# One list scheduler in the source for every engine and every transfer of an attention and feed-forward kernel

## The chip, the core and the metric

The kernel runs on one core of one Trainium2 chip. The metric is the device time of one execution in microseconds (us). The kernel before was run three times: 918.08, 918.18 and 919.11 us, median 918.18. A further execution was recorded by the profiler; every row below is from that one.

## The reference

Eight sequences of 576 tokens with eight heads of 64 go through a sparse attention: heads 0 to 3 look back over 32 tokens, heads 4 to 7 look at every 32nd token. The result, 4608 tokens of 512 values, goes through two matrices with a silu between them.

```python
scores = scale * np.matmul(q, k.transpose(0, 1, 3, 2))
mask_local = (rel >= 0) & (rel < stride)                      # heads 0..3, stride 32
mask_strided = (rel >= 0) & (pos[None, :] % stride == pos[:, None] % stride)
scores = np.where(masks[None, :, :, :], scores, -1000000000.0)
attn = np.exp(scores - np.max(scores, axis=-1, keepdims=True))
attn = attn / (np.sum(attn, axis=-1, keepdims=True) + 1e-09)
x = np.matmul(attn, v)            # then (4608, 512)
h = x @ w_in                      # (512, 2048)
out = (h * (1.0 / (1.0 + np.exp(-h)))) @ w_out
```

## The kernel before

**Attention.** A sequence has six groups, so there are 48 groups, numbered c. Of the six, 0 to 2 are local and 3 to 5 strided. A group goes through these steps, and the text names them by letters: S, the scores (TensorE, L380); M, mask and row minimum (VectorE, L396); E, the exponentials (ScalarE, L403); R, sum and reciprocal (VectorE, L422 and L423), and N, for strided groups only, the scaling of the weights (VectorE, L427); T, the transposition on TensorE (L433); P, its copy out of PSUM (ScalarE, L437); O, the product with the values (TensorE, L445 local, L453 strided). A local group then has Q, a scaling (VectorE, L463), and B, 16 transpositions of 32x32 blocks on VectorE (L499, `blocks`); a strided one has a ScalarE copy (L476). The trace shows two records for one attention matmul, the listed order one.

**Feed-forward.** Numbers are kept in two halves, a rounded high part and a low rest, so each product is three matmuls of 128x128 weights with 512 columns. Tokens come in nine blocks of 512.

- Stage 1 (block 0, to about 138 us): weights come in by 32 pieces and are split; the attention of sequences 0 and 1 runs beside it.
- Stage 2 (blocks 1 and 2, to about 395 us): for each of 16 chunks of the hidden layer there is a hidden step h (12 matmuls into PSUM, L529), then the silu chain tanh on ScalarE (L539), gate (VectorE, L543), high part (L552) and low part (VectorE, L556), and one chunk later the output step o (12 matmuls, L576). Beside it, 18 groups of attention run in bursts, and sums of weight blocks are prepared for stage 3: GpSimd adds two blocks (`summed`, L820, twice) and makes four sums (L825 to L828); ScalarE rounds a half (`halved`, L834), it is stored (L835), VectorE takes the rest (L836), and it is stored (L837); both again for the other half. There are 16 such rounds with one buffer, and each round's parts follow each other. Unchanged weight blocks are stored too (`plain`, L815, six stores of 128 KB a round, 96 in all).
- Stage 3 (blocks 3 to 8 in three pairs, by seven products in place of eight for each layer): 12 matmuls a step (L1044 first layer, L1089 second layer), weights read back in units of 1 MB (`load_unit`, L866), operands built on ScalarE and VectorE (L904, L906, L912, L968, L976), results stored from L1105.

**What sets the order.** In stage 1 a list scheduler in the source (`Steps`, `arrange`) places the steps of all engines by estimated costs and due times. From `others.close()` on, TensorE's and SyncE's queues take the order in which the source is written: in stage 2 h, o, the stores of `prepare`, and where `plan` says so a `burst(c)`, which is T of c+1, S of c+2, O of c. For VectorE, ScalarE and GpSimd the framework chooses the order there. Each engine works off its queue in order.

```python
    def burst(c):
        turn(c + 1)
        scores(c + 2)
        values(c)
        total(c + 2)
```

Of the kernel before, what the change touches and what calls it, by code (L numbers as in the profile page):

```python
# [102 lines left out]
SIGNAL = 0.2  # L103


class Step:
    def __init__(self, name, costs, due, after, act):
        self.name, self.costs, self.due, self.act = name, costs, due, act
        self.engine, self.after = None, list(after)
        self.takes, self.ends, self.place = [], {}, {}  # L110
        self.writes, self.start, self.end = [], None, None


class Steps:
# [3 lines left out]
    def __init__(self):  # L118
        self.all, self.rings, self.by_name = [], {}, {}
        self.readers, self.taken = collections.defaultdict(list), collections.defaultdict(list)  # L120

# [19 lines left out]

    def ready(self, step):

        at = 0.0
        for other in step.after:
            if other.end is None:
                return None
            at = max(at, other.end + (SIGNAL if other.engine != "SP" else LANDING))
        for ring in step.takes:
            if len(self.taken[ring]) >= self.rings[ring]:  # L150
                for other in self.taken[ring][-self.rings[ring]].ends[ring]:
                    if other.end is None:
                        return None
                    at = max(at, other.end + SIGNAL)
        return at

    def arrange(self):
        free = collections.defaultdict(float, SP=1.3, DVE=6.0, ACT=7.6, POOL=6.8)
        left, order = list(self.all), []
        while left:  # L160
            could = []
            for step in left:
                if (at := self.ready(step)) is not None:
                    ways = [(max(free[e], at), e, cost) for e, cost in step.costs.items()]
                    at, engine, cost = min(ways, key=lambda way: way[0] + way[2])
                    could.append((at, step, engine, cost))
            now = min(c[0] for c in could)
            soon = [c for c in could if c[0] <= now + 0.05]
            at, step, step.engine, cost = min(soon, key=lambda c: c[1].due)
            step.start, step.end, step.cost = at, at + cost, cost  # L170
            free[step.engine] = step.end
            for ring in step.takes:
                self.taken[ring].append(step)
            left.remove(step)
            order.append(step)
        return order
# [3 lines left out]
def sparse_attention_ffn(ctx: ExitStack, tc: tile.TileContext, kqt, vt, w_in, w_out, out, out_t):  # L180
# [172 lines left out]
    class Attention:  # L353
# [31 lines left out]
        def peak(self):  # L385
# [7 lines left out]
            for c in range(g.n):  # L393
                for h in range(2):
# [7 lines left out]
                    if not self.quick:  # L402
                        nc.scalar.activation(  # L403
                            out=s_sb[:, c, h], in_=s_sb[:, c, h], func=AF.Exp,
                            bias=nmax[:, c, h : h + 1], scale=-1.0,
                            accum_out=rsum[:, c, h : h + 1],
                        )
# [82 lines left out]
        def blocks(self):  # L490
# [6 lines left out]
            for t, d in itertools.product(range(n), range(n)):  # L497
# [6 lines left out]
    def parts(k, cc):  # L504
        at = k * T
        while at < (k + 1) * T:
            b = at // S
            n = min((b + 1) * S, (k + 1) * T) - at
            if (k, b) == (2, 1):
                yield carry[:, cc, at - k * T : at - k * T + n], slice(at - k * T, at - k * T + n)  # L510
# [225 lines left out]
    for step in steps.arrange():  # L736
        step.act()
    others.close()

    due = [(kind, j) for j in range(2 * NG, len(groups)) for kind in "kv"]  # L740
    due = [what for what in due if what not in (("k", 2 * NG), ("k", 2 * NG + 1))]
    scored, weighed = set(range(2 * NG + 2)), set(range(2 * NG))

    def load_due():

        while due:
            kind, j = due[0]
            bufs, load_one, read = (KBUFS, load_qk, scored) if kind == "k" else (
                VBUFS, load_v, weighed)
            if j - bufs not in read:  # L750
                return
            load_one(groups[j].b, groups[j].gi)
            due.pop(0)
# [3 lines left out]
    def scores(c):  # L757
        if c < len(groups):
            groups[c].scores()
            scored.add(c)  # L760
            load_due()
            groups[c].peak()

    def total(c):
        if c < len(groups):
            groups[c].total()
            if not groups[c].g.local:
                groups[c].scale()

    def turn(c):  # L770
        if c < len(groups):
            groups[c].turn()
            groups[c].turned()

    def values(c):
        if c < len(groups):
            groups[c].values()
            weighed.add(c)
            load_due()
            if groups[c].g.local:  # L780
                groups[c].share()
                groups[c].blocks()
            else:
                groups[c].sorted()
# [14 lines left out]
    ops_dram = [[dram.tile([7, P, 4, 2, Q], F32, name=f"ops{layer}{half}") for half in range(2)]  # L799
                for layer in range(2)]  # L800
    raw = ffn.tile([P, 4, Q], F32, name="stage", bufs=AHEAD - LENT)
    spare = ffn.tile([P, 2, 2, Q], F32, name="stage", bufs=AHEAD - LENT)
    upper = spare[:, 0].bitcast(F32R)
    carry = spare[:, 1].rearrange("p a b -> p (a b)").rearrange("p (c s) -> p c s", c=NP)
    nc.gpsimd.tensor_copy(out=carry, in_=xs[1][:, :, 2 * T - S :])
# [5 lines left out]
    def plain(layer, j):  # L811
        for name, fc, at in (("A11", j, 0), ("A12", j + HALF if layer else j, 0 if layer else Q),
                             ("A22", j + HALF, Q)):
            for half in range(2):
                load(out=where(layer, name, j)[:, half],  # L815
                     in_=weight(layer, half, fc)[:, at : at + Q].bitcast(F32))

    def summed(layer, j):
        for n, fc in enumerate((j, j + HALF)):
            nc.gpsimd.tensor_add(  # L820
                raw[:, 2 * n : 2 * n + 2].rearrange("p a q -> p (a q)"),
                weight(layer, 0, fc).bitcast(F32), weight(layer, 1, fc).bitcast(F32),
            )
        a11, a12, a21, a22 = (raw[:, n] for n in ((0, 2, 1, 3) if layer else (0, 1, 2, 3)))
        nc.gpsimd.tensor_add(a22, a21, a22)  # L825
        nc.gpsimd.tensor_sub(a21, a11, a21)
        nc.gpsimd.tensor_sub(a11, a22, a11)
        nc.gpsimd.tensor_sub(a12, a12, a11)  # L828

    def halved(layer, j, n):  # L830
        kept = ops_dram[layer][j // 4]
        part = raw[:, 2 * n : 2 * n + 2]
        to = kept[3 + 2 * n : 5 + 2 * n, :, j % 4].rearrange("a p h q -> p a h q")
        nc.scalar.copy(out=upper, in_=part)  # L834
        load(out=to[:, :, 0], in_=upper.bitcast(F32))  # L835
        nc.vector.tensor_sub(out=part, in0=part, in1=upper.bitcast(F32))  # L836
        load(out=to[:, :, 1], in_=part)  # L837

    def prepare(k, fc):
        layer, j = k - 1, fc // 2  # L840
        last = (layer, j - 1) if j else (layer - 1, HALF - 1)
        if fc % 2 == 0:
            if last[0] >= 0:
                halved(*last, 1)
            summed(layer, j)
        else:
            plain(layer, j)
            if (layer, j) != (1, HALF - 1):
                halved(layer, j, 0)
# [8 lines left out]
    unit_names = ("w00_5", "w00_9", "w01_12")  # L858
    unit_tiles = {}
    used = [0]  # L860

    def load_unit(n):
# [383 lines left out]
```

## Time and profile before

| | |
|---|---|
| three runs, us | 919.11, 918.08, 918.18 |
| the profiled execution, us | 920.54 |
| its span from first to last instruction, us | 918.8 |
| TensorE busy in the span | 94% |
| VectorE, ScalarE, GpSimd busy | 67%, 50%, 13% |
| mean granted TensorE clock | 0.976 |

The profiled execution took 920.54 us, of which 918.8 lie between its first and its last instruction. A row of the timeline has start, duration, engine, line, operation, tile written and read, shape and count, and in brackets how long the engine sat idle before it and what it then waited for. A row of the windows has the length, then for PE, PEld (its weight loads), DVE (VectorE), ACT (ScalarE) and POOL (GpSimd) the busy time and the number of instructions, then the granted clock (PEclk), the share of time in which the DMA engines were busy, and GB/s. SPq is SyncE issuing transfers.

### The profile page before, as it was taken

Reading aid. Unit: us, or ns where it says so; the run is one execution under the profiler, and the core shown is the slowest. Engines: PE = TensorE matmul, PEld = TensorE weight load, DVE = VectorE, ACT = ScalarE, POOL = GpSimd, SP = SyncE. Lnnn points to the kernel's source line nnn. Section 1 sums busy time; section 2 is a strip of 40 time slices with the busy share of each in tenths; the row PEclk is TensorE's granted clock in tenths of the full one; section 3 lists DMA queues with packets and bytes.
Section 4 is the critical chain, followed back from the end, with each engine's and each line's share of the span. In section 5 each row is a group of like instructions: output and inputs, shape, how many; then the busy total and the mean of one; then the engine's idle time right before and its main releaser. Section 6 shows DMA issues by size and latency. Waiting matters only on the chain.

```text
span 918.8 us, 15147 instructions
## 1 busy us (share of the span) xinstructions
PE 863.4 (94%) x5554; PEld 696.1 (76%) x5554; DVE 612.4 (67%) x1620; ACT 459.6 (50%) x994; POOL 119.4 (13%) x136
## 2 busy tenths in 40 slices
PE   6899999899889889789899999999999999999997
PEld 4687878688668667567678877877888888888886
DVE  7899767844876785717367896747487662168663
ACT  4977634333454334344675466456654443445440
POOL 4101031424434424400000000000000000000000
PEclk9899999999999999878999999999999999999999
DMA  7985515554566555755565565765556466555653
GB/s 226 311 267 190 174 51 171 188 193 147 173 198 195 184 182 185 240 176 181 170 218 201 197 226 202 240 226 198 186 185 216 172 237 229 198 183 188 221 205 119
DMA packets 79626, 180.32 MB, mean 196 GB/s; under 512 B 7872, under 2 KB 56000, under 8 KB 68800
## 3 DMA queue, kind: packets, MB, share of 16 engines
q1 hardware_dynamic: 79552, 179.35, 58.1%
q8 instruction: 44, 0.72, 0.3%
q14 instruction: 30, 0.25, 0.1%
HBM read 140.53 MB, written 38.80 MB: 195 GB/s over the span
## 4 chain that ended last, share of the span: by engine, by line
PE 53%; DVE 6%; DMA 4%; ACT 3%; POOL 2%; issue 1%; SPq 1%; POOLq 0%; ACTq 0%; DVEq 0%
PE z L1089 25%; PE z L1044 24%; DMA ops<-stage 4%; DVE w L499 1%; PE ps L453 1%; DVE xb L499 1%; PE ps L445 1%; PE ps L380 1%; PE po L576 1%; POOL stage L820 1%; DVE sm L396 1%; DVE stage L836 1%; ACT pt L437 1%; ACT stage L834 0%; PE ps L433 0%
## 5 line engine op out<-in xcount | busy, mean ns | idle before, releaser
L1044 PE MATMUL z<-w,w 128*128 128x512 f32 x720 | 169.9, 395 | 0.0
L1044 PEld LDWEIGHTS z<-w,w 128*128 128x128 f32 x720 | 136.6, 191 | 30.4 <-issue 0.9
L529 PE MATMUL ps<-xhi,w 128*128 128x512 f32 x384 | 134.2, 407 | 1.9 <-ACT pt L437 1.9
L1089 PE MATMUL z<-w,w 128*128 128x512 f32 x576 | 134.9, 390 | 0.0
L1089 PEld LDWEIGHTS z<-w,w 128*128 128x128 f32 x576 | 107.7, 188 | 22.7 <-issue 0.2
L403 ACT ACTIVATE sm<-sm,sums 128x64 f32<-128x64 f32 x228 | 77.0, 342 | 26.1 <-DVE sums L396 25.9
L529 PEld LDWEIGHTS ps<-xhi,w 128*128 128x128 f32 x384 | 73.9, 192 | 20.9 <-ACT pt L437 2.1
L529 PE MATMUL ps<-xlo,w 128*128 128x512 f32 x192 | 76.6, 399 | 2.0 <-DVE xlo L521 2.0
L576 PE MATMUL po<-w,g 128*128 128x512 f32 x276 | 71.1, 392 | 1.3 <-DVE g L552 0.9
L380 PE MATMUL ps<-kbd 128*32 128x128 f32 (+1 forms) x928 | 50.2, 299 | 13.9 <-DMA kbd<-kqt 12.0
L576 PEld LDWEIGHTS po<-w,g 128*128 128x128 f32 x276 | 51.3, 188 | 13.9 <-DVE g L552 1.8
L836 DVE TENSOR_TENSOR stage<-stage 128x512 f32<-128x512 f32 x32 | 23.2, 724 | 50.6 <-ACT stage L834 44.8
L834 ACT CAST stage<-stage 128x512 fp32r<-128x512 f32 x32 | 19.8, 619 | 73.9 <-DMA ops<-stage 28.1
L380 PEld LDWEIGHTS ps<-kbd 128*32 128x32 f32 (+1 forms) x928 | 36.7, 128 | 24.2 <-issue 13.9
L499 DVE STREAM_TRANSPOSE xb<-xq 32x96 f32<-32x96 f32 x192 | 51.8, 270 | 2.8
L1089 PE MATMUL z<-xlo,w 128*128 128x512 f32 x216 | 52.0, 390 | 0.0
L1089 PE MATMUL z<-xhi,w 128*128 128x512 f32 x216 | 52.0, 390 | 0.0
L820 POOL TENSOR_TENSOR stage<-w,w 128x512 f32<-128x512 f32 x23 | 35.0, 1524 | 114.9 <-DMA ops<-stage 87.2
L539 ACT ACTIVATE th<-ps 128x512 f32<-128x512 f32 x48 | 28.6, 596 | 41.1 <-PE ps L529 29.6
L968 DVE TENSOR_TENSOR w<-w,w 128x1024 fp32r<-128x1024 f32 (+3 forms) x41 | 44.7, 1104 | 6.4 <-ACT w L976 6.3
L543 DVE SCALAR_TENSOR_TENSOR th<-th,ps 128x512 f32<-128x512 f32 x48 | 32.8, 682 | 23.4 <-ACT th L539 23.3
L1089 PEld LDWEIGHTS z<-xlo,w 128*128 128x128 f32 x216 | 40.5, 188 | 8.6 <-issue 0.2
(171 smaller groups left out, 1497.3 us busy)
## 6 DMA issues: line engine op xcount, KB each, us to landing
w<-ops SPq DMA_DIRECT2D x84, 1024.0 KB, 4.8
ops<-stage SPq DMA_DIRECT2D x64, 256.0 KB, 2.6
vbd<-vt SPq DMA_DIRECT2D x48, 192.0 KB, 3.3
ops<-w SPq DMA_DIRECT2D x65, 128.0 KB, 2.9
stage<-w_in SPq DMA_DIRECT2D x16, 512.0 KB, 4.6
stage<-w_out SPq DMA_DIRECT2D x16, 512.0 KB, 4.6
kbd<-kqt SPq DMA_DIRECT2D x32, 221.0 KB, 3.8
kbd<-kqt SPq DMA_DIRECT2D x32, 208.0 KB, 3.3
```

The source lines that it names most:

```text
L380: nc.tensor.matmul(s_ps[rows, c], kbd[:, 1, g.q0[t] : g.q0[t] + g.rows], kbd[:, 0:3:2, g.k0[t] : g.k0[t] + KW], start=True, stop=True,)
L403: nc.scalar.activation(out=s_sb[:, c, h], in_=s_sb[:, c, h], func=AF.Exp, bias=nmax[:, c, h : h + 1], scale=-1.0, accum_out=rsum[:, c, h : ...
L499: nc.vector.transpose(out=dst[cols, :, rows], in_=src[rows, :, cols])
L529: nc.tensor.matmul(ph, weight(0, wi, fc)[:, cc * P : (cc + 1) * P], x[xi][:, cc], start=(cc, n) == (0, 0), stop=(cc, n) == (NP - 1, 2),)
L539: nc.scalar.activation(out=th[:, cols], in_=ph[:, cols], func=AF.Tanh, scale=0.5)
L543: nc.vector.scalar_tensor_tensor(out=th[:, cols], in0=th[:, cols], scalar=1.0, in1=ph[:, cols], op0=ALU.add, op1=ALU.mult,)
L576: nc.tensor.matmul(po[tt], g[gi][:, cols], weight(1, wi, fc), start=fc == 0 and n == 0, stop=fc == NFC - 1 and n == 2,)
L820: nc.gpsimd.tensor_add(raw[:, 2 * n : 2 * n + 2].rearrange("p a q -> p (a q)"), weight(layer, 0, fc).bitcast(F32), weight(layer, 1, fc).bi ...
L836: nc.vector.tensor_sub(out=part, in0=part, in1=upper.bitcast(F32))
L968: nc.vector.tensor_tensor(out=o, in0=x, in1=y, op=op1)
L1044: nc.tensor.matmul(z[jp][:, jj], w[:, at, wi, cc * P : (cc + 1) * P], op[:, xi, cc], start=fresh and (cc, n) == (0, 0), stop=(cc, n) == (1 ...
L1089: nc.tensor.matmul(z[key][:, ds], w[:, at, wi, ds * P : (ds + 1) * P], op[:, gi, jj], start=fresh and (jp, jj, n) == (0, 0, 0), stop=(jp, ...
```

## The change

The list scheduler now orders everything, and nothing is left to the written order or the framework. Stages 2 and 3 become steps with an engine, a cost, the places they read and write, and the buffers they take. New or changed:

- `do` makes a step and finds what it must follow from the places read and written. `backward` gives due times: it walks the TensorE steps in the order in which they were added, sets their times one after another, and sets every other step early enough for its readers.
- `arrange` takes at each moment the steps that can start first and among those within 0.05 us the one due first. It adds 1.3 us where ScalarE would change its function table.
- The 16 block transpositions B of a local group are four steps of four (`blocks_of`); the exponentials are one step for each column block (`exp_one`).
- The plain stores and the halves of the sums are steps of their own for SyncE, ScalarE and VectorE.
- `change` stands between stages 2 and 3: all steps that use the earlier PSUM pools are placed before it.

The instructions themselves are the same. The diff, cut to its core (line numbers in the order rows of the kernel after are its own):

```diff
+    def do(self, name, costs, act, reads=(), writes=(), due=None, after=(), takes=(), table=None):
+        step = Step(name, costs, due, after, act)
+        for place in reads:
+            step.after += self.writers[place]
+        for place in writes:
+            step.after += self.writers[place] + self.readers[place]
...
+    def backward(self, first, begin):
+        due = {}
+        at = begin
+        for step in self.all[first:]:
+            if "PE" in step.costs:
+                step.due = at
+                at += step.costs["PE"]
+            due[step] = at + 10.0
+        for step in reversed(self.all[first:]):
+            if step.due is None:
+                step.due = due[step] - min(step.costs.values())
+            for other in step.after:
+                if other in due:
+                    far = LANDING + 3.0 if "SP" in other.costs else SIGNAL + 0.5
+                    due[other] = min(due[other], step.due - far)
...
-        def blocks(self):
+        def blocks_of(self, t):
...
-            for t, d in itertools.product(range(n), range(n)):
+            for d in range(n):
...
-    for step in steps.arrange():
-        step.act()
-    others.close()
...
-    def burst(c):
-        turn(c + 1)
-        scores(c + 2)
-        values(c)
-        total(c + 2)
+    def burst(c):
+        add_turn(c + 1)
+        add_scores(c + 2)
+        add_values(c)
+        add_total(c + 2)
...
+                s = do(f"plain{layer}.{j}.{name}{half}", {"SP": 0.7}, go, reads=[("w", layer, fc)],
+                       after=[split_at[layer, fc]])
...
+        do("wh" + name, {"ACT": 0.57}, cast, reads=[f"raw{n}"], writes=["upper"])
+        s0 = do("ws" + name, {"SP": 1.2}, lambda: load(out=to()[:, :, 0], in_=tiles["upper"].bitcast(F32)),
+                reads=["upper"])
+        do("wl" + name, {"DVE": 0.68}, low, reads=["upper"], writes=[f"raw{n}"])
+        s1 = do("wt" + name, {"SP": 1.2},
+                lambda: load(out=to()[:, :, 1], in_=tiles["raw"][:, 2 * n : 2 * n + 2]),
+                reads=[f"raw{n}"])
...
+        h = do("h" + name, {"PE": 2.72}, go, reads=[("w", 0, fc), *(("x", cc) for cc in range(NP))],
+               writes=["ph" + name], after=first, takes=["ps", "ph"])
...
+    changed = do("change", {"POOL": 0.0}, change)
...
+    for step in late_steps:
+        step.behind.append(changed)
...
+    steps.backward(mark, 125.0)
+    for step in steps.arrange():
+        step.act()
```

The first place is VectorE in stage 2, from the end of M of group 16 on. Before (L463 is Q of local group 14, L499 its B, L422, L423 and L427 are R and N of group 16, L836 is a rest of a weight sum, the others are two silu chains):

```order
L463 TENSOR_TENSOR xq<-ps,sums 128x384
L499 STREAM_TRANSPOSE xb<-xq 32x3x32 x16
L422 TENSOR_SCALAR sums<-sums 128x8
L836 TENSOR_TENSOR stage<-stage 128x512
L543 SCALAR_TENSOR_TENSOR th<-th,ps 128x512
L423 RECIPROCAL sums<-sums 128x8
L552 CAST g<-th 128x512
L427 TENSOR_TENSOR sm<-sm,sums 128x4x2x64
L556 TENSOR_TENSOR g<-th,g 128x512
```

And now, in the same place:

```order
L525 TENSOR_TENSOR xq<-ps,sums 128x384
L561 STREAM_TRANSPOSE xb<-xq 32x3x32 x12
L989 TENSOR_TENSOR stage<-stage 128x512
L484 TENSOR_SCALAR sums<-sums 128x8
L485 RECIPROCAL sums<-sums 128x8
L605 SCALAR_TENSOR_TENSOR th<-th,ps 128x512
L489 TENSOR_TENSOR sm<-sm,sums 128x4x2x64
L561 STREAM_TRANSPOSE xb<-xq 32x3x32 x4
L989 TENSOR_TENSOR stage<-stage 128x512
L618 TENSOR_TENSOR g<-th,g 128x512
```

Twelve transpositions still stand ahead of R and N of group 16, and the last four have moved behind them; the high part of the silu chain has gone to ScalarE.

The second place is TensorE beside it. Before, T of group 16 (ident, sm) follows the output step directly, and S of 17 (kbd) and O of 15 (pt, vbd) follow T:

```order
L576 MATMUL po<-w_0_557,g 128x512
L576 MATMUL po<-w_0_539,g 128x512
L433 MATMUL ps<-ident,sm 128x128 x4
L380 MATMUL ps<-kbd_83 64x128 x6
L453 MATMUL ps<-pt,vbd_80 64x54 x16
L529 MATMUL ps<-xhi,w_5_756 128x512
```

And now:

```order
L638 MATMUL po<-w_0_561,g 128x512
L638 MATMUL po<-w_0_543,g 128x512
L440 MATMUL ps<-kbd_83 64x128 x6
L515 MATMUL ps<-pt,vbd_80 64x54 x16
L495 MATMUL ps<-ident,sm 128x128 x4
L591 MATMUL ps<-xhi,w_5_760 128x512
```

S and O have moved ahead of T. In stage 3 the bursts are likewise taken apart: where T, S and O of a burst stood together between two runs of 24 matmuls, now 12 matmuls stand between S and O in most places.

The third place is SyncE's queue in stage 2, up to the load of the keys of group 21 (kbd_83 with 442 columns). Before (L815 are plain stores, L835 and L837 stores of sums, vbd the values of another group):

```order
L815 DMA ops_1625<-w_5_756 128x256
L815 DMA ops_1625<-w_4_719 128x256
L815 DMA ops_1625<-w_13_1211 128x256
L815 DMA ops_1625<-w_12_1146 128x256
L835 DMA ops_1625<-stage 128x2x256
L837 DMA ops_1625<-stage 128x2x256
L341 DMA vbd_79<-vt 64x768 x2
L335 DMA kbd_83<-kqt 64x2x442 x2
L835 DMA ops_1625<-stage 128x2x256
```

And now, from the last plain store of the program on (L951 plain, L993 and L997 sums, L395 keys, L401 values):

```order
L951 DMA ops_164<-stage_1463 128x256
L395 DMA kbd_83<-kqt 64x2x442 x2
L993 DMA ops_162<-stage 128x2x256
L997 DMA ops_162<-stage 128x2x256
L401 DMA vbd_80<-vt 64x768 x2
L993 DMA ops_162<-stage 128x2x256
L997 DMA ops_162<-stage 128x2x256
L395 DMA kbd_82<-kqt 64x2x442 x2
```

The keys now stand ahead of the stores of sums. All 96 plain stores have moved forward: 32 stand before the last weight piece of stage 1, 53 before the first store of a sum, and the last one at the keys of group 21, the eighth of the 18 groups whose scores stage 2 computes.

More of the change, by code (lines that the diff above doesn't have):

```diff
@@ L171, in arrange @@
             free[step.engine] = step.end
+            if step.engine == "ACT" and step.table:
+                table = step.table
             for ring in step.takes:
                 self.taken[ring].append(step)
-            left.remove(step)
+            ready.remove(step)
             order.append(step)
+            for other in then[step]:
+                waits[other] -= 1
+                if not waits[other]:
+                    opened(other)
+                    ready.append(other)
         return order
@@ L757, in scores @@
[L757 to L784, printed above, removed]
+    ops_dram = [[dram.tile([7, P, 4, 2, Q], F32, name=f"ops{layer}{half}") for half in range(2)]
+                for layer in range(2)]
@@ new lines, in add_total, with add_turn @@
+    def add_total(c):
+        if c >= len(groups):
+            return
+        a = groups[c]
+        n = a.g.n
+        parts = [f"sm{c}.{i}" for i in range(n)]
+        r = do(f"R{c}", {"DVE": 0.45}, a.total, reads=parts, writes=[f"sum{c}"])
+        if not a.g.local:
+            r = do(f"N{c}", {"DVE": 0.08 + 0.14 * n}, a.scale, reads=[f"sum{c}"], writes=parts)
+            steps.ends(steps[f"M{c}"], "sum", [r])
+    def add_turn(c):
+        if c >= len(groups):
+            return
+        a = groups[c]
+        n = a.g.n
+        parts = [f"sm{c}.{i}" for i in range(n)]
+        late = c + 1 >= late_from
+        t = do(f"T{c}", {"PE": 0.1 + 0.11 * n}, a.turn, reads=parts, writes=[f"psp{c}"],
+               takes=["ps1" if late else "ps"])
+        (late_steps if late else early_steps).append(t)
+        p = do(f"P{c}", {"ACT": 0.05 + 0.13 * n}, a.turned, reads=[f"psp{c}"],
+               writes=[f"pt{c}"], takes=["pt"])
+        steps.ends(t, t.takes[0], [p])
+        steps.ends(steps[f"M{c}"], "sm", [t, steps[f"R{c}"]])
@@ L830, in halved, with go @@
[L830 to L837, printed above, removed]
+                def go(name=name, fc=fc, at=at, half=half):
+                    load(out=where(layer, name, j)[:, half],
+                         in_=weight(layer, half, fc)[:, at : at + Q].bitcast(F32))
@@ L1002, in pair, with add_pair @@
+    zs = itertools.count()
+    def add_pair(p, bursts):
         k = SINGLE + 2 * p
         n0 = 35 * p
[L1004 to L1015 removed]
@@ L1017, in then @@
-        def then(n, needs, act):
-            made.append((n, act))
+        x_op = x_ops(p)
         step = [0]
+        queue = [(35 * p + 7 + m, m // 4, m % 4) for m in range(28)]
+        made_ops = [0]
         def stepped():
-            if p == 0 and step[0] < 2:
-                halved(1, HALF - 1, step[0])
             for c in bursts.get(step[0], ()):
@@ new lines, in add_pair, with after_op @@
+            stepped()
+    spent = set()
+    todo = [n for n in range(OPS, 35 * PAIRS)]
+    def after_op(p, n):
+        spent.add(n)
+        while todo and todo[0] - OPS in spent:
+            q, m = divmod(todo[0], 35)
+            if m >= 7:
+                i, jp = divmod(m - 7, 4)
+                if f"A{q}.{6 if i else 4}.{jp}" not in steps.by_name:
+                    return
+                g_op(q, i, jp)
+            elif m != 3:
+                x_ops(q)(m)
+            todo.pop(0)
@@ L1155, in sparse_attention_ffn @@
-            output(*lag, po)
+                pass
             if fc == 0:
-                store(k - 1, po)
-                po = [ps_o.tile([P, DM], F32, name="po") for _ in range(NTT)]
+                add_output(k - 1, NFC - 1)
+                add_store(k - 1)
+            else:
+                add_output(k, fc - 1)
             prepare(k, fc)
```

776 lines of the change are left out of this document (529 added, 247 removed).

## The prediction

> **What bounds the kernel now.** I read the page first, then the windows by stage, the waits of TensorE, and the timeline where the long waits lie. TensorE is the bound, but its 94% say little about where the rest can be had. The windows cut the span where stage 1 ends (137.9), at the first matmul of stage 3 (395), after the last attention (722) and after the last matmul (913.7).
>
> ```profile
> core 0: us, PE busy (x) PEld busy (x) DVE busy (x) ACT busy (x) POOL busy (x), PEclk, DMA share, GB/s
> 0.00:137.90 137.90, 124.68 (x1033) 98.07 (x1034) 112.14 (x367) 90.09 (x162) 25.47 (x46) 0.98 0.63 203
> 137.90:395.00 257.10, 234.11 (x1671) 185.92 (x1670) 177.72 (x601) 106.74 (x364) 93.92 (x90) 0.95 0.57 186
> 395.00:722.00 327.00, 313.02 (x1990) 253.76 (x1988) 216.21 (x555) 181.92 (x384) 0.00 (x0) 0.98 0.59 202
> 722.00:913.70 191.70, 191.62 (x865) 158.36 (x864) 105.14 (x99) 80.82 (x85) 0.00 (x0) 1.00 0.56 198
> 913.70:918.80 5.10, 0.00 (x0) 0.00 (x0) 1.18 (x1) 0.00 (x0) 0.00 (x0) 0.94 0.26 103
> ```
>
> From 722 on TensorE never stops and its clock is full: nothing to gain there, nor in the 5.1 us of the last store. Idle are 23.0 us of stage 2 (257.1 less 234.1) and 14.0 of stage 3's first part (327.0 less 313.0). How long the work itself takes at full clock comes from two places: the chain of waits has a run of 336 matmuls without a break, and the timeline shows an unhindered burst (T, S, O) from its first start to that of the next hidden step.
>
> ```profile
> 837.46 76.17 PE z L1089 x336
> ```
> ```profile
> 156.44 0.49 PE L433 MATMUL ps<-ident,sm 128*128 128x128 f32 x3
> ...
> 158.68 0.50 PE L529 MATMUL ps<-xhi,w 128*128 128x512 f32 x1
> ```
>
> A matmul takes 76.17/336 = 0.2267 us, a step of twelve 2.72, a burst 2.24. Stage 2 has 32 hidden steps and 33 output steps, 65 x 2.72 = 176.8, and 18 bursts, 40.3: 217.1 us of work in 257.1. So 40.0 are lost, 23.0 idle and 17.0 in slow matmuls. Stage 3's first part has 168 steps less the 70 that fit into the window after it, 98 x 2.72 = 266.6, and 17 bursts, 38.1: 304.7 in 327.0, so 22.3 lost, 14.0 idle and 8.3 slow. What TensorE waits for, stage 2 and then the first part of stage 3:
>
> ```profile
> PE ps L380 <- DMA kbd<-kqt: 6.3, 3, 2.8
> PE po L576 <- DVE g L552: 6.2, 3, 4.6
> PE ps L433 <- DVE sm L427: 4.9, 2, 2.4
> PE po L576 <- DVE g L556: 2.0, 2, 1.5
> ```
> ```profile
> PE ps L445 <- ACT pt L437: 5.7, 6, 2.7
> PE ps L433 <- DVE sm L427: 2.8, 2, 1.9
> PE ps L453 <- DVE sums L396: 2.3, 2, 1.2
> PE ps L453 <- ACT pt L437: 1.7, 4, 0.4
> ```
>
> No cause holds a large part. They have one thing in common: an instruction that TensorE needs stands in its queue behind one that is long or itself waits.
>
> **Part one: T behind the long transpositions.** Of the four waits for N (L427) this is the first, on VectorE:
>
> ```profile
> 173.74 4.52 DVE L499 STREAM_TRANSPOSE xb<-xq 32x96 f32<-32x96 f32 x16
> ...
> 180.03 0.69 DVE L427 TENSOR_TENSOR sm<-sm,sums 128x512 f32<-128x512 f32 x1
> ```
> ```profile
> 170.31 0.60 PE L433 MATMUL ps<-ident,sm 128*128 128x128 f32 x4
> 170.85 1.10 PE L380 MATMUL ps<-kbd 128*64 128x128 f32 x16
> ...
> 180.86 1.03 PE L433 MATMUL ps<-ident,sm 128*128 128x128 f32 x4 [2.44 <-DVE sm L427]
> ```
>
> From the end of S of group 16 (171.9) to T at 180.86 it took 8.9 us, of which the transpositions took 4.52. The new order puts twelve of them ahead of R and N, 3.4 us, and leaves a silu rounding to ScalarE, so N ends more than 1.1 us earlier; and S and O, nearly 2 us of a burst's 2.24, stand ahead of T. Together that covers the 2.44. The row at 180.86 shows the second half of the price: T takes 1.03 instead of the 0.60 at 170.31. Slow matmuls follow a wait, and I let them go with it.
>
> [...]
>
> **Part two: keys and sums on SyncE.**
>
> ```profile
> 218.17 3.06 SPq L815 DMA_DIRECT2D ops<-w  x6
> 227.44 0.37 SPq L835 DMA_DIRECT2D ops<-stage  x1
> ```
> ```profile
> 234.44 1.09 PE L380 MATMUL ps<-kbd 128*64 128x128 f32 x16 [2.84 <-DMA kbd<-kqt]
> ```
>
> The keys of group 21 stood behind a store of sums that could not go before 227.44, and TensorE waited 2.84 us for them. The new order has them ahead of it. The plain stores, 0.5 us of the queue each, leave the second half of stage 2 altogether. That shortens the rounds of sums:
>
> ```profile
> 160.08 0.73 POOL L825 TENSOR_TENSOR stage<-stage 128x256 f32<-128x256 f32 x1
> ```
> ```profile
> 278.72 2.15 DMA ops<-stage
> ...
> 287.10 1.31 POOL stage L820
> ...
> 341.05 6.03 DMA ops<-stage
> ```
>
> A round is one L820 (1.3), four sums of 0.73 (3.2 with the gaps between), two roundings and a rest (0.6 each; the rest's row, L836, is below, and a rounding is taken alike), two stores to their landing, and, estimated, 0.5 of hand-offs: 6.8 plus two landings. With 2.15 that is 11.1 us, with 6.03 it is 18.9. Stage 2 at the forecast below gives a round 230/16 = 14.4 us, so the rounds keep ahead as long as a landing stays under 3.8. The 6.03 came straight behind six plain stores; I take landings near 2.15 to 2.6 for most.
>
> What the stores meet instead is stage 1. There 32 of them go between the weight pieces; the transfers were busy for 0.63 of that stage, TensorE for 124.7 of its 137.9 us. A store is 0.5 us of SyncE, and a piece is asked for six pieces ahead. I take 0.5 us, between nothing and 3 us (six stores of 0.5 in a row, as at 218.17, ahead of one piece that is needed).
>
> **Part three: the end of stage 2.**
>
> ```profile
> 377.22 0.69 DVE L556 TENSOR_TENSOR g<-th,g 128x512 fp32r<-128x512 f32 x1
> ...
> 385.87 1.07 DVE L906 TENSOR_TENSOR xhi<-xb,xhi 128x384 fp32r<-128x384 f32 x1
> ...
> 389.22 0.69 DVE L836 TENSOR_TENSOR stage<-stage 128x512 f32<-128x512 f32 x1 [1.42 <-POOL stage L828]
> 389.83 0.68 DVE L556 TENSOR_TENSOR g<-th,g 128x512 fp32r<-128x512 f32 x1
> 390.44 0.82 DVE L906 TENSOR_TENSOR xhi<-xb,xhi 128x640 fp32r<-128x640 f32 x1
> ```
> ```profile
> 375.33 0.60 ACT L539 ACTIVATE th<-ps 128x512 f32<-128x512 f32 x1 [3.36 <-DVE g L556]
> ```
> ```profile
> 387.86 1.22 PE L576 MATMUL po<-stage,g 128*128 128x512 f32 x2 [4.55 <-DVE g L552]
> 390.57 4.63 PE L576 MATMUL po<-stage,g 128*128 128x512 f32 x10 [1.50 <-DVE g L556]
> ```
>
> Operands for stage 3 (L906) and a rest of a sum (L836) that waited for GpSimd stood ahead of the last low part (389.83): 6.05 us idle, and ten matmuls took 4.63 instead of 2.27. Now only one operand's rest, 1.07 + 0.82 in two pieces, stands between the chain's high and low part. The chain before it ran unhindered from 375.33 to 377.91, 2.6 us; with that rest it takes 4.5 against the 2.72 of the output step ahead: 1.8 us are left of the 8.4.
>
> **Part four: bursts in stage 3.** O needs the PSUM buffer that P frees, and P runs on ScalarE; the waits for P are 7.4 us in ten. Twelve matmuls (2.72 us) now stand between S and O, more than nine of the ten waits. The two waits of up to 1.9 for N there and the two of 1.2 for M are covered in the same way where other matmuls fill in; at two places I see less than a microsecond left (N of group 34, and a third PSUM tile that waits for the gate before it).
>
> **The sum.** Going by the causes, I would remove most of 62.3. A static order meets its estimates only roughly, though, and a late instruction can no longer be passed by another. I let a third stay, 13.3 in stage 2 and 7.4 in stage 3's first part, which has room for the 1.8 above and a dozen new waits of a microsecond or so. The gain is 26.7 + 14.9 - 0.5 = 41.1. Against the span that gives 918.8 - 41.1 = 877.7. The profiled execution took 920.54 with its 1.7 around the span, 2.4 more than the median of the three runs, so I take the gain from the median: 918.2 - 41.1 = **877** us. If a tenth of the loss stays, the gain is 36.0 + 20.1 and the time 862; if two thirds stay, it is 13.3 + 7.4 - 3 and 900. What I find likely of the forecast's own case is 866 to 890.
>
> **The rivals.**
>
> Rival 1, VectorE becomes the pace between local groups. In stage 2 it works 177.7/18 = 9.9 us a group, TensorE 217.1/18 = 12.1. Half the groups are local and have B, 4.5, where the others have N, 0.7, so a local one costs 1.9 more than the mean, 11.8. Beside GpSimd the silu chain's operations stretch:
>
> ```profile
> 315.52 1.03 DVE L552 CAST g<-th 128x512 fp32r<-128x512 f32 x1
> 316.58 1.10 DVE L556 TENSOR_TENSOR g<-th,g 128x512 fp32r<-128x512 f32 x1
> ...
> 339.15 0.43 DVE L552 CAST g<-th 128x512 fp32r<-128x512 f32 x1
> ```
>
> That is 1.0 more a chain, of which the mean holds a part; with 1.78 chains a group, all beside GpSimd, a local group comes to 13 us and more, over TensorE's 12.1. If each of the nine local groups then leaves 2 us of waiting and 1 us of slow matmuls, 27 of stage 2's 40.0 stay: gain 13.0 + 14.9 - 0.5 = 27.4, time 891 (884 to 899). Against it: VectorE is busy 177.7 of 257.1 as a whole, and GpSimd 93.9. Chance 0.18.
>
> Rival 2, the slow matmuls do not go with the waits. Only the idle third to two thirds can be had: two thirds of 37.0 is 24.7, less 0.5, time 894. [...] Against it stand the rows at 170.31 and 180.86. Chance 0.05.
>
> Rival 3, slower than before: the rounds of sums become the pace, because their roundings and rests now stand at fixed places in ScalarE's and VectorE's queues, and the silu chains behind them. At 6.03 us a landing, a round of 18.9 x 16 makes stage 2 302 us, 45 longer, less 14.9 and plus 0.5: 949. It turns the whole slower once a round passes (257.1 + 14.4)/16 = 17.0, a landing of 5.1. Against it: 2.15 is seen as often as no plain stores stand ahead. Chance 0.04.
>
> Rival 4, nothing moves, because the waits follow data and not the order: 918. The rows of part one speak against it. Chance 0.03.
>
> **How the numbers follow.** The forecast has 0.70: 877. Rivals 1 and 2 are faster too, so faster by more than 0.2% (1.8 us, about what a measurement of this kernel can tell from no change) is 0.70 + 0.18 + 0.05 = 0.93, within it 0.03, slower 0.04. The range 866 to 897 takes in nine tenths of the forecast's case and most of rivals 1 and 2, some 0.8 in all; the forecast's own is 866 to 890.
>
> **What would show it.** In the profile after: stage 2 from its first hidden step to the first matmul of stage 3 in about 230 us, stage 3's first part in about 312, the rest as before; no wait of T for N above 1 us in stage 2; no wait for keys above 1 us; stores of sums landing under 3 us; under 2 us of wait at the last output step; a mean granted clock above 0.985. It is wrong if stage 1 is over 3 us longer, if ScalarE or VectorE wait for the sums and the silu chains stand behind that, or if the waits go and the matmuls stay slow.

## The result, and the profile after

The changed kernel takes 879.3 us (median of four runs, 877.1 to 881.1) where the kernel before takes 918.6 (918.1 to 919.9) beside it: a ratio of 0.957, with a 95% interval of 0.954 to 0.960. The forecast was 877, and 866 to 897. The profiled execution took 881.1, of which 879.3 are its span.

The windows of the changed kernel, cut where the work is the same as in the kernel before: the first T of group 12, the first matmul of stage 3, a place in its second half, the last matmul. The columns are the prediction's.

```profile
0.00:143.07 143.07, 127.24 (x1031) 98.23 (x1032) 110.13 (x359) 92.57 (x166) 27.49 (x47) 0.98 0.81 253
143.07:370.05 226.98, 222.66 (x1673) 179.42 (x1672) 183.76 (x599) 112.58 (x372) 91.84 (x89) 0.99 0.55 177
370.05:682.00 311.95, 310.70 (x2012) 249.16 (x2011) 215.50 (x555) 181.59 (x385) 0.00 (x0) 1.00 0.59 210
682.00:874.20 192.20, 191.47 (x844) 157.77 (x842) 104.43 (x98) 80.27 (x84) 0.00 (x0) 1.00 0.55 197
874.20:879.30 5.10, 0.01 (x1) 0.00 (x0) 1.23 (x1) 0.00 (x0) 0.00 (x0) 0.92 0.26 103
```

The kernel before is cut for this at the same T:

```profile
137.66 0.49 PE L433 MATMUL ps<-ident,sm 128*128 128x128 f32 x3
```

Stage 2 took 257.3 and takes 227.0: 30.4 us less. Stage 3 up to the last matmul took 518.7 and takes 504.2: 14.5 less. Stage 1 took 137.7 and takes 143.1: 5.4 more. 30.4 + 14.5 - 5.4 = 39.5, which is the difference of the spans, 918.8 - 879.3. In stage 2 TensorE is idle for 4.3 us instead of 23.0, and its 222.7 us of busy time are 5.6 over the work of 217.1, where it was 17.0: the clock column went from 0.95 to 0.99 with the waits. What TensorE still waits for, in stage 2 and then in the first 312 us of stage 3:

```profile
PE po L638 <- DVE g L618: 2.0, 2, 1.6
PE ps L495 <- DVE sm L489: 1.1, 2, 0.8
PE ps L591 <- DVE sums L484: 0.5, 1, 0.5
PE ps L495 <- ACT g L614: 0.5, 2, 0.3
```
```profile
PE z L1386 <- DVE w L1299: 0.7, 1, 0.7
PE z L1424 <- DMA w<-ops: 0.5, 1, 0.5
```

The waits for keys (6.3 us), for the high parts (6.2) and for P (7.4) are gone, and those of T for N are 1.1 in stage 2, where they were 4.9, and none in stage 3, where they were 2.8. Group 16, the place of part one, in VectorE's queue and then in TensorE's:

```profile
181.78 3.38 DVE L561 STREAM_TRANSPOSE xb<-xq 32x96 f32<-32x96 f32 x12
...
186.67 0.68 DVE L489 TENSOR_TENSOR sm<-sm,sums 128x512 f32<-128x512 f32 x1
187.38 1.13 DVE L561 STREAM_TRANSPOSE xb<-xq 32x96 f32<-32x96 f32 x4
```
```profile
185.52 0.88 PE L440 MATMUL ps<-kbd 128*64 128x128 f32 x12
186.22 1.09 PE L515 MATMUL ps<-pt,vbd 128*64 128x54 f32 x32
187.50 0.63 PE L495 MATMUL ps<-ident,sm 128*128 128x128 f32 x4 [0.18 <-ACT g L614]
```

N stands behind twelve transpositions and before four, S and O stand ahead of T, and T waits 0.18 us instead of 2.44. The end of stage 2, TensorE:

```profile
360.64 3.80 PE L638 MATMUL po<-stage,g 128*128 128x512 f32 x14
366.06 4.15 PE L638 MATMUL po<-stage,g 128*128 128x512 f32 x10 [1.61 <-DVE g L618]
```

The one wait of stage 2 above a microsecond is where the prediction left 1.8 us, at the last output step, and it is 1.61. Its price is higher than that: the ten matmuls behind it take 4.15 us, 1.9 over their 2.27.

Stage 1 is the part that went against the forecast. These are the transfers between 55 and 120 us: their busy share in 40 slices, in tenths; the queue's packets, MB and share; and the weight pieces and plain stores issued, with their size and the median us from issue to landing. Before:

```profile
DMA  4995898889949423000897765069456910759400
...
q1 hardware_dynamic: 7379, 12.20, 58.6%
...
stage<-w_out SPq DMA_DIRECT2D x9, 512.0 KB, 3.8
stage<-w_in SPq DMA_DIRECT2D x8, 512.0 KB, 4.3
```

And after:

```profile
DMA  8999789899699899673399889798259969994687
...
q1 hardware_dynamic: 11943, 16.24, 83.1%
...
stage<-w_out SPq DMA_DIRECT2D x9, 512.0 KB, 5.5
ops<-w SPq DMA_DIRECT2D x33, 128.0 KB, 5.1
stage<-w_in SPq DMA_DIRECT2D x8, 512.0 KB, 5.2
```

The 17 pieces are the same, and 33 plain stores have joined them, 29 of them ahead of the last piece. They fill the slices that were empty, but also those that were full already, and a piece now takes 0.9 to 1.7 us longer from its issue to its landing. The stores bring a third more bytes (16.24 MB for 12.20) and take 42% more of the transfers' time (83.1 for 58.6%).

### The profile page after: what moved, and what is told of

It is laid out like the page before. It is cut to its first block, busy times and chain, and to the rows that moved or that the text cites. A ratio compares the mean times of both kernels' runs of the same rounds, so it can differ in the third digit from the quotient of the medians.

```text
span 879.3 us, 15187 instructions
## 1 busy us (share of the span) xinstructions
PE 852.1 (97%) x5554; PEld 684.6 (78%) x5554; DVE 615.0 (70%) x1608; ACT 467.0 (53%) x1006; POOL 119.3 (14%) x136
## 4 chain that ended last, share of the span: by engine, by line
PE 73%; DVE 13%; DMA 7%; ACT 3%; POOL 2%; issue 2%; SPq 0%; POOLq 0%; ACTq 0%; DVEq 0%
PE z L1386 26%; PE z L1424 25%; PE po L638 7%; PE ps L591 7%; PE ps L440 4%; DMA stage<-w_in 2%; PE ps L515 2%; DMA w<-ops 2%; DVE g L618 2%; DVE xb L561 2%; DVE w L561 1%; PE ps L495 1%; DVE sm L456 1%; DVE th L605 1%; DMA kbd<-kqt 1%
## 5 line engine op out<-in xcount | busy, mean ns | idle before, releaser
L1386 PEld LDWEIGHTS z<-w,w 128*128 128x128 f32 x720 | 134.2, 188 | 31.4 <-issue 1.1
L591 PE MATMUL ps<-xhi,w 128*128 128x512 f32 x384 | 131.1, 399 | 2.3 <-ACT pt L499 1.4
L1424 PEld LDWEIGHTS z<-w,w 128*128 128x128 f32 x576 | 107.4, 188 | 24.0 <-DMA w<-ops 1.0
L591 PEld LDWEIGHTS ps<-xhi,w 128*128 128x128 f32 x384 | 72.0, 188 | 21.0 <-issue 1.7
L465 ACT ACTIVATE sm<-sm,sums 128x64 f32<-128x64 f32 x228 | 77.3, 345 | 15.3 <-DVE sums L456 15.2
L440 PE MATMUL ps<-kbd 128*32 128x128 f32 (+1 forms) x928 | 48.4, 294 | 6.5 <-POOL mask_strided L287 5.6
L1424 PEld LDWEIGHTS z<-xhi,w 128*128 128x128 f32 x216 | 40.1, 188 | 8.4 <-issue 0.2
L605 DVE SCALAR_TENSOR_TENSOR th<-th,ps 128x512 f32<-128x512 f32 x48 | 32.5, 677 | 19.1 <-ACT th L601 18.9
L618 DVE TENSOR_TENSOR g<-th,g 128x512 fp32r<-128x512 f32 x48 | 43.8, 912 | 1.7 <-ACT g L614 0.8
```

Of the source, the lines that this page charges most:

```text
L440: nc.tensor.matmul(s_ps[rows, c], kbd[:, 1, g.q0[t] : g.q0[t] + g.rows], kbd[:, 0:3:2, g.k0[t] : g.k0[t] + KW], start=True, stop=True,)
L465: nc.scalar.activation(out=self.s_sb[:, c, h], in_=self.s_sb[:, c, h], func=AF.Exp, bias=self.nmax[:, c, h : h + 1], scale=-1.0, accum_out ...
L591: nc.tensor.matmul(ph, weight(0, wi, fc)[:, cc * P : (cc + 1) * P], x[xi][:, cc], start=(cc, n) == (0, 0), stop=(cc, n) == (NP - 1, 2),)
L605: nc.vector.scalar_tensor_tensor(out=th[:, cols], in0=th[:, cols], scalar=1.0, in1=ph[:, cols], op0=ALU.add, op1=ALU.mult,)
L618: nc.vector.tensor_sub(out=g[1][:, cols], in0=th[:, cols], in1=g[0][:, cols].bitcast(F32))
L1386: nc.tensor.matmul(zt[z][:, jj], w[:, at, wi, cc * P : (cc + 1) * P], op[:, xi, cc], start=fresh and (cc, n) == (0, 0), stop=(cc, n) == (1 ...
```

## The experiments

The theory to be tested: TensorE waited because an instruction that it needed stood in another engine's queue (VectorE's above all, and SyncE's) behind one that was long or waited itself, and the scheduler's order put these first. The main rival: TensorE's own order does it, with other matmuls between the parts of a burst. The instructions are the same as before, but not all on the same engine: of the 48 roundings to the high part VectorE makes 24 and ScalarE 24, where it was 39 and 9. The runs e3, e9 and e10 below keep that split, so they give the price of order alone, and what the shift is worth was not tried. Besides, the cause of the 5.4 us in stage 1, the cut of the transpositions, and the price of a round of sums were each tried by themselves. All stages in us, from the profiled executions, cut as above; the kernel before runs beside each.

| kernel | median | range | stage 1 | stage 2 | stage 3 |
|---|---|---|---|---|---|
| before | 918.6 | 918.1 to 919.9 | 137.7 | 257.3 | 518.7 |
| after | 879.3 | 877.1 to 881.1 | 143.1 | 227.0 | 504.2 |
| e0 after again | 880.1 | 878.8 to 881.9 | 144.2 | 226.3 | 504.5 |
| e1 plain stores late | 877.4 | 876.2 to 878.0 | 139.1 | 226.4 | 503.8 |
| e2 TensorE as written | 891.3 | 891.2 to 894.7 | 142.0 | 232.8 | 510.7 |
| e3 VectorE, ScalarE, GpSimd free | 912.4 | 908.2 to 915.2 | 143.3 | 249.5 | 514.6 |
| e4 a quarter of each plain store early | 884.0 | 882.4 to 885.5 | 138.5 | 226.4 | 510.6 |
| e5 plain stores from GpSimd's queue | 887.9 | 887.8 to 888.5 | 142.1 | 230.4 | 508.0 |
| e6 two more sums in a round | 898.6 | 898.0 to 899.5 | 142.6 | 245.3 | 504.7 |
| e7 four more sums in a round | 938.5 | 937.8 to 939.6 | 147.1 | 281.0 | 503.5 |
| e8 sixteen transpositions in one | 879.5 | 878.3 to 880.3 | 143.5 | 226.6 | 503.1 |
| e9 VectorE alone free | 897.9 | 897.0 to 901.0 | 142.9 | 237.9 | 513.4 |
| e10 ScalarE alone free | 885.6 | 883.4 to 887.4 | 142.1 | 229.8 | 506.6 |
| e11 e1 and e8 together | 878.6 | 877.1 to 880.8 | 140.0 | 228.5 | 503.0 |

### e0: the changed kernel again

> The changed kernel once more, as the measure for the runs beside it. All theories: 877 to 881 us, the same stages as in its profile (143.1 to the first hidden step of stage 2, 227 for stage 2, 504 for stage 3).

It came as expected, with 144.2 us of stage 1 and the other two stages within 0.7 us of the first profile: the stages can be compared to about a microsecond.

### e1: the plain stores late

```
                 s = do(f"plain{layer}.{j}.{name}{half}", {"SP": 0.7}, go, reads=[("w", layer, fc)],
-                       after=[split_at[layer, fc]])
+                       after=[split_at[layer, fc], steps["p31"]])
```

> The plain stores go only after the last weight piece has been asked for; nothing else is changed in the source. Theory one (the 5.4 us that stage 1 grew are pieces that come late because plain stores stand ahead of them in SyncE's queue and among the transfers): stage 1 ends near 138, its new waits at the high and low parts go, stage 2 stays within 1 us of 227, the time is about 874. Theory two (stage 1 grew because of the new order on VectorE and ScalarE): stage 1 stays near 143, the time near 879. Theory three (the stores are dearer in stage 2, behind the keys and the sums): stage 1 gains 5, stage 2 loses as much or more, with waits for keys or for sums that land late; 879 or above.

Stage 1 went back to 139.1 and stage 2 stayed at 226.4: theory one, with 1.4 us of stage 1 still above the 137.7 of the kernel before. The pieces between 55 and 120 us land as before:

```profile
stage<-w_out SPq DMA_DIRECT2D x9, 512.0 KB, 4.3
stage<-w_in SPq DMA_DIRECT2D x8, 512.0 KB, 4.0
...
ops<-w SPq DMA_DIRECT2D x5, 128.0 KB, 5.5
```

By the two profiles the gain is 5.7 us of span; by the medians of the runs on the same chip, 2.8 (877.4 against 880.1, and the ranges do not meet). I hold to the smaller figure, since the two profiled executions are the fastest of one kernel's four and the slowest of the other's. In stage 2 the plain stores cost nothing measurable, though their freedom there was the reason to move them forward.

### e4 and e5: what in the plain stores delays the pieces

SyncE's queue time, or the transfers? In e4 each plain store is cut in two; a quarter of its columns goes in the old place, the rest after the last piece:

```
+                for part, (a, b) in enumerate(((0, Q // 4), (Q // 4, Q))):
...
+                           after=[split_at[layer, fc]] + [steps["p31"]] * part)
```

> Each plain store is cut in two: a quarter of its columns goes where the changed kernel has the store, the other three quarters after the last weight piece. SyncE has as many stores between the pieces as in the changed kernel, the transfers a quarter of their bytes there; in stage 2 SyncE has more stores. Theory one (the pieces come late because SyncE issues plain stores ahead of them, 0.5 us each): stage 1 stays at 142 to 144. Theory two (the pieces come late because the stores take the transfers' time: 0.81 of stage 1 busy for 0.63): stage 1 goes back to 138 to 140, with the piece's landing back near 4.6 us. Stage 2 is expected within 3 us of 227 by both.

In e5 the stores keep their places and bytes, and GpSimd's queue issues them:

```
-                    load(out=where(layer, name, j)[:, half],
+                    nc.gpsimd.dma_start(out=where(layer, name, j)[:, half],
```

> The plain stores keep their places in the order and their bytes, but GpSimd's queue issues them instead of SyncE's. Theory one (SyncE's queue delays the pieces): stage 1 ends near 139. Theory two (the transfers delay them): stage 1 stays at 142 to 144, with pieces that take 5.2 us and more to land. By both, stage 2 may grow, where GpSimd issues stores beside its sums.

The same stretch of e4, then of e5:

```profile
stage<-w_out SPq DMA_DIRECT2D x9, 512.0 KB, 4.5
stage<-w_in SPq DMA_DIRECT2D x8, 512.0 KB, 4.3
ops<-w SPq DMA_DIRECT2D x32, 32.0 KB, 3.5
```
```profile
ops<-w POOLq DMA_DIRECT2D x38, 128.0 KB, 5.0
stage<-w_out SPq DMA_DIRECT2D x9, 512.0 KB, 4.9
stage<-w_in SPq DMA_DIRECT2D x7, 512.0 KB, 5.4
```

About as many stores of a quarter of the bytes, in the same queue, leave stage 1 at 138.5; the whole bytes from another queue leave it at 142.1. So it is the transfers' time that delays the pieces, and SyncE's issuing has 1 or 2 us of it at most (142.1 against the 143.1 and 144.2 of the changed kernel's two profiles). Of the two runs e4 is the clearer one, since e5 has 38 stores in the stretch instead of 33. As a whole both kernels are slower than the changed one. What e5 loses in stages 2 and 3 was not taken apart. In e4 the loss is in stage 3, 6 us longer, where the new order has made a wait of its own:

```profile
PE z L1387 <- ACT osb L1056: 4.9, 1, 4.9
```

### e2: TensorE's order as written

```
+    line = [step for step in steps.all[mark:] if "PE" in step.costs]
+    for one, two in zip(line, line[1:]):
+        two.behind.append(one)
```

> TensorE's steps after stage 1 keep the order in which the source builds them, as in the kernel before; all other engines and SyncE are still ordered by the scheduler. Theory one (the gain comes from what stands in the other engines' queues ahead of the instruction that TensorE waits for): most of the gain stays, 885 to 895, and the waits that come back are those that only a later place on TensorE covers (T directly behind S, O behind P). Theory two (the gain comes from TensorE's own order, other matmuls between the parts of a burst): most of the gain goes, 905 to 918. From the causes of the kernel before, I expect theory one to hold for stage 2 and theory two for the waits for P in stage 3.

It lost 11.2 of the 37.0 us that lay between before and after on this chip (917.1 and 880.1): 6.5 in stage 2 and 6.2 in stage 3. TensorE's waits of the whole program now have these:

```profile
PE ps L495 <- DVE sm L489: 4.2, 5, 1.5
...
PE ps L507 <- ACT pt L499: 3.4, 6, 1.2
...
PE ps L515 <- ACT pt L499: 2.1, 5, 0.4
```

Those are the waits of T for N and of O for P, which stood in the kernel before and which part four let other matmuls cover. So theory one holds for most of the gain, and theory two for its rest.

### e3, e9 and e10: the other engines' order

From the end of stage 1 on, e3 leaves the order of VectorE, ScalarE and GpSimd to the rules of the kernel before; in e9 that is VectorE alone, in e10 ScalarE alone, by a line that holds the other two (here e9's). TensorE's and SyncE's orders are the scheduler's in all three.

```
+    early_ones = set(steps.all[:mark])
     for step in steps.arrange():
         step.act()
+        early_ones.discard(step)
+        if early_ones is not None and not early_ones:
+            others.close()
+            ctx.enter_context(tc.manual_schedule(engines={getattr(mybir.EngineType, e) for e in ("Activation", "Pool")}))
...
```

> TensorE and SyncE keep the scheduler's order; VectorE, ScalarE and GpSimd are ordered by it only in stage 1, and after that go by the rules of the kernel before. Theory one (the order of the other engines carries the gain): most of it goes, 900 to 915, with waits for N, for the gates and for sums as before. Theory two (TensorE's order carries it): 879 to 885. If both this run and the one with TensorE as written keep over half of the gain, each order alone covers the same waits.

> TensorE, SyncE, ScalarE and GpSimd keep the scheduler's order to the instruction; only VectorE goes by the rules of the kernel before from the end of stage 1 on. Theory one (VectorE's queue carries what the run with all three free lost, 32 us): 900 to 912, with waits of T for N as there. Theory two (ScalarE's queue, where th and P stand behind other work, carries most): 880 to 888.

> The mirror of the run beside it: only ScalarE goes by the rules of the kernel before from the end of stage 1 on, VectorE and all others by the scheduler's order. Theory one: 880 to 890. Theory two: 900 to 912, with waits for gates and high parts that ScalarE rounds. If both runs lose a large part, the two queues need each other's order: 890 to 905 each.

e3 lost 32.3 of the 37.0 us. Its TensorE waits for N again:

```profile
342.42 1.08 PE L495 MATMUL ps<-ident,sm 128*128 128x128 f32 x4 [3.08 <-DVE sm L489]
```

And its VectorE shows why, as the kernel before did at 173.74:

```profile
334.59 3.38 DVE L561 STREAM_TRANSPOSE w<-xq 32x96 f32<-32x96 f32 x12
338.00 1.13 DVE L484 TENSOR_SCALAR sums<-sums 128x8 f32<-128x8 f32 x1
339.16 1.13 DVE L561 STREAM_TRANSPOSE w<-xq 32x96 f32<-32x96 f32 x4
...
341.59 0.68 DVE L489 TENSOR_TENSOR sm<-sm,sums 128x512 f32<-128x512 f32 x1
```

R and N, which T needs, stand between and behind transpositions that nobody needs yet. At the end of its stage 2, TensorE waits for a low part, and in the last output step for the high part, as in the kernel before:

```profile
375.65 2.56 PE L638 MATMUL po<-stage,g 128*128 128x512 f32 x10 [1.53 <-DVE g L618]
386.87 1.22 PE L638 MATMUL po<-stage,g 128*128 128x512 f32 x2 [3.22 <-DVE g L614]
```

With VectorE alone free (e9) the loss is 17.8 against e0's median, with ScalarE alone (e10) 5.4 (another chip; the kernel before took 918.7 there and 917.1 beside e0). The longest wait of T for N is 4.0 us in e9 and 2.4 in e10. All three free lose more than these two by themselves, 32.3 against 23.2. So of the two VectorE's queue carries the most; that a place which one of them loses is still covered in part by the other's order would explain the difference, but was not shown, and GpSimd was not freed alone. Nor does a run give SyncE its old order back: that its new one removed the waits for keys is read from the profiles, where they are gone after stage 1 in the changed kernel and in e3 alike.

### e8 and e11: the transpositions as one step

```
-        xs_ = [do(f"B{c}.{t}", {"DVE": 1.1}, lambda t=t: a.blocks_of(t), reads=[f"xq{c}"], after=to)
-               for t in range(P // STRIDE)]
+        xs_ = [do(f"B{c}", {"DVE": 4.4}, lambda: [a.blocks_of(t) for t in range(P // STRIDE)],
+                  reads=[f"xq{c}"], after=to)]
```

> The long transpositions of a group with blocks are one step of sixteen again (4.4 us) instead of four of four; the scheduler orders the whole anew with that. Theory one (the prediction's part one: T waits for N behind 4.5 us of transpositions, and the cut lets R, N and the silu chains between them): waits of T for N and of output steps for the high and low parts come back in part, stage 2 is 5 to 12 us longer, 885 to 892. Theory two (the order round them is enough, with S and O and other matmuls ahead of T): within 2 us of 880.

Theory two: 879.5, and stage 2 as with four steps. VectorE and TensorE at group 16:

```profile
183.25 4.51 DVE L561 STREAM_TRANSPOSE xb<-xq 32x96 f32<-32x96 f32 x16
...
190.36 0.69 DVE L489 TENSOR_TENSOR sm<-sm,sums 128x512 f32<-128x512 f32 x1
```
```profile
188.02 1.09 PE L515 MATMUL ps<-pt,vbd 128*64 128x54 f32 x32
191.90 0.60 PE L495 MATMUL ps<-ident,sm 128*128 128x128 f32 x4
```

N ends 3.0 us after O's start (191.05 and 188.02), where it is 1.1 in the changed kernel (187.35 and 186.22), and T does not wait: it starts 3.9 us after O instead of 1.3, and a hidden step of twelve matmuls has come between them. The scheduler was told of the 4.4 us and could cover them. The cut is worth nothing that can be measured here.

> Both edits that cost nothing or gained: plain stores after the last weight piece, and the long transpositions as one step. If the two stand apart: stage 1 ends near 139, stage 2 takes 226 to 227, the time is 874 to 878, as with the late plain stores alone. If the sixteen transpositions in a row need the slack that the plain stores take from SyncE in stage 2, stage 2 grows by some microseconds: 879 to 885.

878.6 lies between what was expected of two edits that stand apart (874 to 878) and of two that do not (879 to 885), with 2 us more in stage 2 than e1 or e8. Its range overlaps those of both, so this stays open. By its median e1 is the fastest kernel of this case: 0.956 of before (0.954 to 0.958).

### e6 and e7: the price of a round of sums

```
-                nc.gpsimd.tensor_add(
...
+                for _ in range(1 + 2 * n):
+                    nc.gpsimd.tensor_add(
...
```

In e7 it is `1 + 4 * n`.

> Every second sum of two weights on GpSimd (L961) is made three times instead of once, to the same end: 2 x 1.30 = 2.6 us more in each round of sums, 16 rounds; the order and the costs in the scheduler stay. Theory one, the prediction's bound (a round is 6.8 us and two landings, of 2.3 us now: 11.4; stage 2 gives it 227/16 = 14.2): a round becomes 14.0, stage 2 grows by 0 to 4 us, the time is 879 to 884. Theory two (the order fixes each round's place in the queues of ScalarE, VectorE and SyncE, so a later round is waited for at once): stage 2 grows by 16 x 2.6 = 42 us, the time is about 920. Theory three (rounds run ahead of what needs them and the stores wait for nobody): no change.

> As the run beside it, with every second sum made five times: 5.2 us more in each round. Theory one: a round becomes 16.6, stage 2 16 x 16.6 = 266, 39 more than now, the time about 918. Theory two: stage 2 grows by 83, the time is about 962. Theory three: no change in TensorE's time, only later stores; below 885. The difference of the two runs, 16 x 2.6 = 42 us where the rounds set the pace, is the price of a us in a round.

A round's length can be read from the first and the last start of its first sum, 15 rounds apart, in the groups of GpSimd's operations on these tiles. The changed kernel, e6 and e7:

```profile
L971 POOL TENSOR_TENSOR stage<-stage x16: 727/740/1068, 131.0 to 360.7; 128x256 f32<-128x256 f32 x16
```
```profile
L972 POOL TENSOR_TENSOR stage<-stage x16: 733/1061/1257, 133.5 to 380.9; 128x256 f32<-128x256 f32 x16
```
```profile
L972 POOL TENSOR_TENSOR stage<-stage x16: 724/737/1070, 138.1 to 421.9; 128x256 f32<-128x256 f32 x16
```

That is 229.7/15 = 15.3 us now, 247.4/15 = 16.5 in e6 and 283.8/15 = 18.9 in e7. The sums of which every second was repeated (L962) take 1.44 us each on the mean in both profiles, more than the 1.30 of the expectation, so 2.9 us were added to a round in e6 and 5.8 in e7. From e6 to e7 a round grew by 2.4 of these further 2.9 us and the median by 39.8: at that point rounds are the pace, at 39.8/2.43 = 16.4 us of time for each us of a round. Without what was added, e7's round is 18.92 - 5.75 = 13.2 and e6's 16.49 - 2.88 = 13.6. So none of the three theories got the two right: e6 was to cost 0 to 4 us by the prediction's bound and 42 by its rival, and cost 18.5; e7, at 938.5, lies between the 918 and the 962. The bound's form was right, but a round is 13.2 to 13.6 long where I had 11.4; only about 2 us of room are left in the 15.3. Where the 2 us more than 11.4 lie was not taken apart. The scheduler was not told of the longer sums, so this is the room of one fixed order.

## Why the prediction was right, and where it was wrong

**Stage 2.** The forecast let a third of the 40.0 lost us stay, 13.3; 9.9 stayed, 4.3 idle and 5.6 in slow matmuls. Gain 30.4 for 26.7.

**Stage 3.** 14.5 for 14.9.

**Stage 1, the step that failed.** The prediction took 0.5 us, between nothing and 3, for plain stores between the weight pieces, and named a stage 1 over 3 us longer as a sign of being wrong. It is 5.4 longer in the profile. Most of that is the stores: e1 gets back 2.8 by the medians and 5.0 by the stages of e1 and e0, and stage 1 takes 139.2 on the mean of e1, e4 and e11, where the stores go late or with a quarter of their bytes, against 143.0 in the changed kernel, e0, e2, e3, e8, e9 and e10, 3.8 more. The 0.8 to 2.3 us by which e1, e4 and e11 stay above the 137.7 of the kernel before were not taken apart. The step priced a store by SyncE's queue, 0.5 us of it each, and took the transfers' 0.63 for room. e4 and e5 show that the queue was the smaller part: the stores share the transfers with the pieces, whose landing grows by 0.9 to 1.7 us. The 0.63 was a mean over a stretch in which, as the slices above show, full ones stand beside empty ones; the likely reading, which no run shows by itself, is that pieces are in flight in the full ones, and lose there what a store takes.

**Part one** had the right wait and half of the reason. The T of group 16 waits 0.18 for 2.44, but the cut of the transpositions, which I counted first, does nothing measurable (e8); a later place for T does it as well.

**Part two.** No wait for keys is left in stage 2, and the stores of sums land in 2.3 us (median) for 2.6. But a round is 13.2 to 13.6 long, so Rival 3, which I gave 0.04, was nearer than it looked. By e6 and e7 the whole becomes as slow as before at a round of 16.5 + (918.6 - 898.6)/16.4 = 17.7. With two landings in a round, that is estimated as a landing of 2.3 + (17.7 - 13.4)/2 = 4.4 us (13.4 lies between the two), where I had 5.1. In e7 it is past that point, with 938.5.

**Part three** said 1.8 us; it is 1.61 and 1.9 in slow matmuls behind it. **Part four** said that matmuls between S and O would cover the waits for P; they are gone, and e2 shows them back.

**The rivals.** Rival 1, VectorE as the pace of local groups, did not come: T waits for N for 1.1 us in all of stage 2. Rival 2, that slow matmuls do not go with the waits, is refuted by the clock: 0.95 to 0.99 in stage 2, and back at 0.93 in that of e7, where the waits are back:

```profile
147.12:428.10 280.98, 240.25 (x1672) 187.66 (x1671) 205.76 (x603) 111.52 (x373) 176.18 (x150) 0.93 0.44 143
```

Rival 4 is refuted by the time and by e3. That the total came within 2.3 us owes something to errors that cancel: 3.7 more in stage 2, 0.4 less in stage 3, 4.9 more lost in stage 1.

## What to carry to other kernels

Where an engine is busy for 90% and waits a little for many things, look in the queues of its suppliers for what stands ahead of the instruction that it needs; here, without the suppliers' order, 32 of 37 us were lost, and VectorE's mattered most. A static order is only as good as its slack: find a loop with little of it (here the rounds of sums, about 2 us of 15) and measure that by making it longer. And when stores are moved into idle queue time, price them by their bytes against the transfers of that very stretch, not by the issuing time: here stage 1 took 138.5 us with a quarter of the bytes in the same places of the same queue (e4), and 143.1 with all of them.

## What the runs showed of the hardware

Short waits can cost their length again. These are the windows of the changed kernel around the wait of 1.61 us at 366.06:

```profile
364.40:366.00 1.60, 0.05 (x1) 0.00 (x0) 1.60 (x4) 0.00 (x0) 0.00 (x0) 1.00 0.83 318
366.00:370.00 4.00, 3.94 (x10) 3.13 (x11) 3.53 (x7) 2.73 (x5) 0.00 (x0) 0.57 0.34 125
```

The granted clock is 0.57 for the next 4 us, and the ten matmuls there take 4.15 us, 1.9 over their 2.27. In the kernel before, the 4 us after the waits of 2.44 us at 180.86 and at 340.32 and of 2.84 at 234.44 have 0.57, 0.63 and 0.64. In e3 a wait of 3.08 us, at 342.42, was followed by 0.56 (342.40 to 346.00), while one of 1.79, at 191.24, was followed by a full clock, 1.00 from 191.20 to 195.00. So a wait of 1.61 us cost clock and one of 1.79 did not: the length of a wait alone does not decide it, and what does was not shown.
